# An attention and gated-MLP kernel: the order of work written by a recorder with a clock, and score banks refilled one by one

## The chip, the cores and the metric

One core of a Trainium2 chip. The metric is device time in microseconds, the median of several executions. Engine names as in the profile: PE is TensorE (PEld its weight loads), ACT is ScalarE, DVE is VectorE, POOL is GpSimd, SP is SyncE. All times in us unless marked ns.

## The reference

```
x  [1, 2048, 512] bf16;  wq [512, 32*16], wk, wv [512, 16], wo [512, 512], w1 [512, 1792], w2 [1792, 512]
xn = layernorm(x)
q  = (xn @ wq) as 32 heads of 16;  k = xn @ wk;  v = xn @ wv        # one k and one v for all heads
p  = softmax(q k^T / sqrt(16))                                      # [32, 2048, 2048]
s  = (p v, heads side by side) @ wo
g  = silu(silu(xn @ w1) @ w2)
out = x + s * g
```

The 32 x 2048 x 2048 exponentials are the bulk of the work. The second input called x is not used.

## The kernel before

The 2048 queries are four chunks (`c`) of 512; the 32 heads are eight groups (`g`) of four. A *group* below is one of the 32 pairs (c, g). Keys come in 16 tiles of 128 (`kt`). A *block* is one head's scores for one key tile and one chunk, transposed: 128 keys x 512 queries, one PSUM bank in fp32. So a key tile of a group has four blocks, one for each head `i`.

**Scores.** A head has 16 channels, so a block is a matmul that uses 32 of the array's 128 rows (L509); matmuls of different `i` run side by side. Two blocks at a time go into `psA0` or `psA1` (two banks each).

**Two ways to an exponential.** Most blocks are done by ScalarE: one ACTIVATE Exp of 128 x 1024, two blocks, from `psA` into `pa_sb` (L568). The others, called dense here, go by VectorE: a TENSOR_SCALAR adds a constant to the scaled score and clamps at zero, and the int16 result, read as bf16, is a coarse exponential, the first *pattern* (`ph0`, L581). GpSimd then makes two shifted patterns from it by INT64_ADD on four int16 at once (`ph1`, `ph2`, L592), and the three patterns together, each with its own weight, are the finer exponential.

**Values.** For each block of ScalarE's and each pattern, a matmul with 32 columns (16 value channels, and ones for the denominator) accumulates into `psO` (L628); four of them, one for each head, run side by side. When a group is complete, VectorE transposes `psO` (L663), takes the reciprocal (L668), multiplies (L674, into `onb_sb`) and, for every second group, transposes back (L679).

**The dense layer.** Matmuls for the MLP (L759, L771), the queries of later chunks (L393) and the output projection (L782) are *jobs* on the single bank `psF`. MLP results pass through a tanh on ScalarE (L817, `t_sb`) and a multiply on VectorE (L858), the output through L866 and the final add of x (L824), then a store on SP's queue. `warm` and `filler` (L268, L805) issue matmuls of zeros where TensorE would otherwise be idle.

**The order.** `Sched.op` records each operation with what it reads and writes; from that it derives the semaphores. Each engine executes its own list strictly in the order recorded. The order is a fixed pattern, written out by hand: `units` are ScalarE's key tiles, two exponentials each (`emit_E`), `dtiles` are the dense ones. A unit with a dense half takes two blocks of a dense tile, together, in `psD` (banks D and D1, one TENSOR_SCALAR of 128 x 1024 in `emit_P1`), and after the second half `emit_shift` issues GpSimd's two adds. After each score pack a rule chooses between a few packs of value matmuls (`emit_PV`) and a part of a job (`emit_job`, two or three matmuls). VectorE's small tasks are let in by `run_dve_task` as far as `room` allows: 0.85 us a unit, or 1.3 with a tanh, by the costs in `COST`, and tasks `gn3` (L674) and `add` (L824) only in every second unit:

```
while room > 0:
    k = run_dve_task(2 * u - 2, [t for t in ANY if COST[t] <= room and not (ph == 0 and t in ("gn3", "add"))])
    room -= COST.get(k, 9)
```

The first `NFRONT` = 12 units (24 exponentials) have no dense half; between them the normalisation and k and v of the later chunks are done. `x_sb` holds all 16 tiles of x from the start to the final add. The pattern buffers have three slots (`NPD`, `NPS`), `pa_sb` has eleven (`NPA`).

Of the kernel before, what the change touches and what calls it, by code (L numbers as in the profile page):

```python
# [35 lines left out]
class Sched:  # L36

    def __init__(self):
        self.queues = {}
        self.done = {}
        self.clock = {}
        self.snap = {}
        self.last_w = {}
        self.readers = {}
        self.flagged = {}
        self.lanes = {}

    def op(self, eng, fn, reads=(), writes=(), lane=None):
        who = lane or eng
        if lane:
            self.lanes[lane] = eng
        n = self.done.get(who, 0)
        self.done[who] = n + 1
# [15 lines left out]
        for w in writes:  # L72
            if w in self.last_w:
                dep(*self.last_w[w])
            for f, m in self.readers.get(w, {}).items():
                dep(f, m)
        clk = self.clock.setdefault(eng, {})
# [61 lines left out]
def bass_recurrent_scan__grouped_kv_mqa__dense_activation_silu__prompt_kernel(  # L139
# [25 lines left out]
    NPD = 3  # L165
# [6 lines left out]
    LEAD = 1  # L172
    NFRONT = 12

    with ExitStack() as es:
# [18 lines left out]
        ph_sb = [sb(f"ph{j}_sb", [P, NPD if j == 0 else NPS, 4 * NQ], I16) for j in range(NPH)]  # L194
# [37 lines left out]
        def load_x(a, b, queue="sp"):  # L232
            op(queue, lambda e: e.dma_start(x_sb[:, a:b, :], xv[:, a:b, :]), writes=[("x", t) for t in range(a, b)],  # L233
               lane=f"lx{a}")
# [7 lines left out]
        op("sp", lambda e: e.dma_start(wq_sb[:], A_wq.rearrange("(dc p) n -> p dc n", p=P)), writes=["wq"], lane="lwq")  # L242
# [22 lines left out]
        def warm(n, bank, key):  # L265
            def f(e):
                for _ in range(n):
                    r = e.matmul(bank, lhsT=zero_sb[:, 0:P], rhs=zero_sb[:, :], start=True, stop=True)  # L268
                return r
            op("pe", f, reads=["zero"], writes=[key])  # L270
# [119 lines left out]
        def mm_Q(c, t, dcs=range(NDC)):  # L390
# [5 lines left out]
            op("pe", f, reads=xnT_keys(c) + ["wq"], writes=["F"])  # L396

        def evac_Q(c, t, eng):
# [3 lines left out]
            else:  # L402
                op("v", lambda e: e.tensor_scalar(dst, psF[:, :], QSCALE, None, op0=ALU.mult), reads=["F"], writes=[("qT", c % 2, t)])
# [86 lines left out]
        units, dtiles = [], []  # L490
        for c in range(NC):
            for g in range(NG):
                n = 0
                while n < NKT and NFRONT + 2 * (len(dtiles) + n + 1) <= len(units) + (NKT - n - 1) - LEAD:
                    n += 1
                units += [(c, g, kt) for kt in range(NKT - n)]
                dtiles += [(c, g, kt) for kt in range(NKT - n, NKT)]
        NU = len(units)
        first_unit = [min(u for u, k in enumerate(units) if k[0] == c) for c in range(NC)]
        for u, k in enumerate(units):  # L500
            phase = (u - NFRONT) % 2
            m = (u - NFRONT) // 2
            d = dtiles[m] if u >= NFRONT and m < len(dtiles) else None
            units[u] = dict(phase=phase, pair=m, A=[[(k, 0), (k, 1)], [(k, 2), (k, 3)]][::1 if phase == 0 else -1],
                            D=[] if d is None else [(d, 0), (d, 1)] if phase == 0 else [(d, 2), (d, 3)])

        def score(e, blk, ap):
            (c, g, kt), i = blk
            return e.matmul(ap, lhsT=kT_sb[g % 2][32 * i:32 * i + 32, kt * P:(kt + 1) * P],  # L509
                            rhs=qT_sb[32 * i:32 * i + 32, c % 2, g // 2, :],  # L510
                            start=True, stop=True, tile_position=(32 * i, 0))

        def burst(items, writes):
            rd = set()
            for ((c, g, kt), i), _ in items:
                if ("q", c, g // 2) not in jst["q"]:
                    raise ValueError(f"no q for {c}, {g}")
                rd.add(("qT", c % 2, g // 2))
                rd.add(("kT", 1, kt // 2, i) if g % 2 else ("kT", 0, kt // 2 if kt else "first"))

            def f(e):
                for blk, ap in items:
                    r = score(e, blk, ap)
                return r
            op("pe", f, reads=sorted(rd, key=str), writes=writes)

        def emit_S(u, which):

            un = units[u]
            burst([(blk, psA[which][:, 512 * k:512 * k + 512]) for k, blk in enumerate(un["A"][which])], ["A%d" % which])  # L530
            if which == 1 and un["D"]:
                burst([(blk, psD[:, 512 * k:512 * k + 512]) for k, blk in enumerate(un["D"])], ["D", "D1"])

        NGRP = NC * NG
        pend = [[] for _ in range(NGRP)]
        left = [0] * NGRP
        for un in units:
            for blk in un["D"]:
                left[blk[0][0] * NG + blk[0][1]] += NPH
            for h in range(2):  # L540
                for blk in un["A"][h]:
                    left[blk[0][0] * NG + blk[0][1]] += 1
        npv = [[0] * 4 for _ in range(NGRP)]
        tot = [[0] * 4 for _ in range(NGRP)]
        for un in units:
            for blk in un["D"]:
                tot[blk[0][0] * NG + blk[0][1]][blk[1]] += NPH
            for h in range(2):
                for blk in un["A"][h]:
                    tot[blk[0][0] * NG + blk[0][1]][blk[1]] += 1  # L550

        step_now = [0]
        state = dict(g=0, o_step=-1, half=0)

        def fresh(key):
            for q in pend:
                for p in q:
                    if p["key"] == key:
                        raise ValueError(f"{key} is still to be read, step {step_now[0]}")

        def emit_E(u, h):
            un = units[u]
            if not un["A"][h]:
                return
            sl = (2 * u + h) % NPA
            step_now[0] = 2 * u
            fresh(("pa", sl))
            op("a", lambda e: e.activation(pa_sb[:, sl, :], psA[h][:, :], ACT.Exp, scale=ESCALE),  # L568
               reads=["A%d" % h], writes=[("pa", sl)])
            for k, (kk, i) in enumerate(un["A"][h]):  # L570
                gi = kk[0] * NG + kk[1]
                pend[gi].append(dict(i=i, kt=kk[2], v=0, ap=pa_sb[:, sl, 512 * k:512 * k + 512], key=("pa", sl),
                                     ready=2 * u + h))

        def emit_P1(u):
            un = units[u]
            if not un["D"]:
                return
            sl, h = un["pair"] % NPD, un["phase"]
            fresh(("ph", 0, sl, h))  # L580
            op("v", lambda e: e.tensor_scalar(ph_sb[0][:, sl, 1024 * h:1024 * h + 1024], psD[:, :],  # L581
                                              float(PH_ONE + PH_BIAS), 0.0, op0=ALU.add, op1=ALU.max),
               reads=["D", "D1"], writes=[("ph", 0, sl, h)])
            for k, (kk, i) in enumerate(un["D"]):
                ap = ph_sb[0][:, sl, 1024 * h + 512 * k:1024 * h + 512 * k + 512].bitcast(BF16)
                pend[kk[0] * NG + kk[1]].append(dict(i=i, kt=kk[2], v=1, ap=ap, key=("ph", 0, sl, h), ready=2 * u + 1))

        def emit_shift(u):
            sl, ss = units[u]["pair"] % NPD, units[u]["pair"] % NPS
            for j in range(1, NPH):  # L590
                fresh(("ph", j, ss))
                op("gp", lambda e, j=j: e.int64_add(ph_sb[j][:, ss, :].bitcast(I64), ph_sb[0][:, sl, :].bitcast(I64),  # L592
                                                    PH_SHIFT[j] * 0x0001000100010001),
                   reads=[("ph", 0, sl, 0), ("ph", 0, sl, 1)], writes=[("ph", j, ss)])
                for h in range(2):
                    for k, (kk, i) in enumerate(units[u - 1 + h]["D"]):
                        ap = ph_sb[j][:, ss, 1024 * h + 512 * k:1024 * h + 512 * k + 512].bitcast(BF16)
                        pend[kk[0] * NG + kk[1]].append(dict(i=i, kt=kk[2], v=1 + j, ap=ap, key=("ph", j, ss),
                                                             ready=2 * (u + 1) + j))

        def emit_PV(step, cap, may_end=True):
            gi = state["g"]
            if gi >= NGRP or step <= state["o_step"]:
                return 0
            n = 0
            while n < cap:
                cand = sorted((p for p in pend[gi] if p["ready"] <= step), key=lambda p: p["ready"])
# [6 lines left out]
                last = left[gi] <= sum(1 for _ in cand)  # L614
# [393 lines left out]
```

## Time and profile before

| | |
|---|---|
| median of 3 runs | 696.4 (695.93 to 697.16) |
| profiled execution, first to last instruction | 695.3 |
| ScalarE busy | 677.0, 97% |
| TensorE busy | 677.3, 97% (6279 matmuls) |
| VectorE busy | 552.4, 79% |
| GpSimd busy | 352.3, 51% |
| granted TensorE clock | 1.000 |
| HBM traffic | 6.85 MB read, 2.10 MB written |

The profile gives the span of one execution; what a timed run has beyond it is the difference of the first two rows, 1.1. Busy time counts an engine as busy while at least one of its instructions is in flight. Matmuls overlap and their ends are modelled, so TensorE's 97% says little of its reserve; its start-to-start distances say more. ScalarE and VectorE instructions overlap too, by a part of their length.

### The profile page before, as it was taken

The numbers are of one execution on the slowest core, as the hardware profiler recorded it, in microseconds if no ns is written. First come the engines' busy times: TensorE is split into PE (matmuls) and PEld (weight loads), VectorE is DVE, ScalarE is ACT, GpSimd is POOL, SyncE is SP. The second block draws the span as 40 slices with busy tenths as digits, with TensorE's granted clock in tenths as the row PEclk, the third lists the DMA queues.
The fourth block names the chain that finished last, engine by engine and source line by source line (L and its number), as shares of the span: only waits on it lengthen the run. The fifth ranks groups of instructions, "written<-read, shape, count | busy, mean of one in ns | idle before, by whom it ended". The sixth has DMA issues, their size and how long they took to land.

```text
span 695.3 us, 14435 instructions
## 1 busy us (share of the span) xinstructions
PE 677.3 (97%) x6279; PEld 183.0 (26%) x6279; DVE 552.4 (79%) x639; ACT 677.0 (97%) x773; POOL 352.3 (51%) x361
## 2 busy tenths in 40 slices
PE   8999999999999999999999999999999999999996
PEld 3432222222222222222222222222222222222221
DVE  6778778887778877888778787887878888787884
ACT  5899999999999999999999999999999999999995
POOL 4134545545455555555555555455545555555452
PEclk9999999999999999999999999999999999999999
DMA  9300000000000000000000000000000000000000
GB/s 296 112 5 1 1 2 1 1 1 2 1 1 8 9 1 9 8 2 1 1 1 10 8 8 1 10 1 1 1 2 1 8 17 2 9 1 2 1 1 31
DMA packets 7887, 10.13 MB, mean 15 GB/s; under 512 B 1744, under 2 KB 7120, under 8 KB 7824
## 3 DMA queue, kind: packets, MB, share of 16 engines
q1 hardware_dynamic: 6656, 5.15, 2.4%
q0 software_dynamic: 736, 3.67, 1.5%
q8 instruction: 49, 0.80, 0.5%
q10 hardware_dynamic: 432, 0.39, 0.2%
q14 instruction: 14, 0.11, 0.1%
HBM read 6.85 MB, written 2.10 MB: 13 GB/s over the span
## 4 chain that ended last, share of the span: by engine, by line
ACT 93%; PE 4%; DVE 1%; DMA 1%; POOL 0%; SPq 0%; issue 0%; DVEq 0%
ACT pa_sb L568 87%; ACT t_sb L817 5%; DMA wq_sb<-in_A_wq_dram 1%; PE psA L509 1%; PE psF L268 1%; PE psD L316 1%; DVE stats_sb L277 0%; PE psO L628 0%; POOL rstd_sb L286 0%; PE psD L351 0%; PE psF L351 0%; PE psA L939 0%; SPq L233 0%; PE psF L771 0%; DVE wq_sb L960 0%
## 5 line engine op out<-in xcount | busy, mean ns | idle before, releaser
L568 ACT ACTIVATE pa_sb<-psA 128x1024 bf16<-128x1024 f32 x692 | 660.5, 1233 | 4.3 <-PE psA L509 3.8
L592 POOL INT64_ADD ph_sb<-ph_sb x332 | 340.5, 1038 | 306.0 <-DVE ph_sb L581 306.0
L581 DVE TENSOR_SCALAR ph_sb<-psD 128x1024 int16<-128x1024 f32 x332 | 405.3, 1221 | 97.6 <-PE psD L509 96.5
L628 PE MATMUL psO<-ph_sb,vaug_sb 128*32 128x512 bf16 x1992 | 236.4, 384 | 0.0
L628 PE MATMUL psO<-pa_sb,vaug_sb 128*32 128x512 bf16 x1384 | 208.9, 384 | 0.4 <-ACT pa_sb L568 0.4
L509 PE MATMUL psA<-qT_sb,kTa_sb 32*128 32x512 bf16 x700 | 135.7, 384 | 4.5 <-ACT pa_sb L568 3.4
L509 PE MATMUL psA<-qT_sb,kTb_sb 32*128 32x512 bf16 x684 | 132.7, 385 | 3.5 <-ACT pa_sb L568 2.5
L509 PEld LDWEIGHTS psA<-qT_sb,kTa_sb 32*128 32x128 bf16 x700 | 32.9, 90 | 152.4 <-ACT pa_sb L568 146.5
L509 PEld LDWEIGHTS psA<-qT_sb,kTb_sb 32*128 32x128 bf16 x684 | 32.1, 91 | 152.0 <-ACT pa_sb L568 150.1
L628 PEld LDWEIGHTS psO<-ph_sb,vaug_sb 128*32 128x32 bf16 x1992 | 53.0, 94 | 58.1 <-issue 45.1
L759 PE MATMUL psF<-xnT_sb,w_sb 128*128 128x512 bf16 x224 | 67.8, 384 | 0.0
L509 PE MATMUL psD<-qT_sb,kTb_sb 32*128 32x512 bf16 x340 | 66.0, 384 | 0.0
L771 PE MATMUL psF<-w_sb,u_sb 128*128 128x512 bf16 x224 | 65.0, 384 | 0.0
L509 PE MATMUL psD<-qT_sb,kTa_sb 32*128 32x512 bf16 x324 | 62.8, 385 | 0.0
L628 PEld LDWEIGHTS psO<-pa_sb,vaug_sb 128*32 128x32 bf16 x1384 | 49.2, 94 | 43.9 <-issue 33.3
L817 ACT ACTIVATE t_sb<-psF 128x512 bf16<-128x512 f32 x72 | 59.3, 824 | 0.0
L858 DVE SCALAR_TENSOR_TENSOR u_sb<-t_sb,psF 128x512 bf16<-128x512 bf16 x56 | 38.3, 684 | 20.6 <-ACT t_sb L817 20.6
L268 PE MATMUL psF<-zero_sb 128*128 128x512 bf16 x100 | 34.3, 413 | 1.2 <-DVE zero_sb L252 1.2
L663 DVE STREAM_TRANSPOSE otr_sb<-psO 128x512 f32<-128x512 f32 x32 | 22.9, 715 | 5.4 <-PE psO L628 5.0
L771 PEld LDWEIGHTS psF<-w_sb,u_sb 128*128 128x128 bf16 x224 | 14.1, 97 | 25.6 <-issue 21.5
L393 PE MATMUL psF<-xnT_sb,wq_sb 128*128 128x512 bf16 x64 | 19.2, 384 | 1.1 <-DMA wq_sb<-in_A_wq_dram 1.1
L759 PEld LDWEIGHTS psF<-xnT_sb,w_sb 128*128 128x128 bf16 x224 | 12.7, 97 | 25.4 <-issue 24.7
(83 smaller groups left out, 222.6 us busy)
## 6 DMA issues: line engine op xcount, KB each, us to landing
w_sb<-in_B_w_dram POOLq DMA_DIRECT2D x2, 1792.0 KB, 12.9
out_dram<-ob_sb SPq DMA_DIRECT2D x15, 128.0 KB, 1.7
x_sb<-in_A_x_dram SPq DMA_DIRECT2D x3, 512.0 KB, 8.2
wq_sb<-in_A_wq_dram SPq DMA_DIRECT2D x1, 512.0 KB, 7.9
wop_sb<-in_A_wo_dram SPq DMA_DIRECT2D x1, 512.0 KB, 10.3
x_sb<-in_A_x_dram SPq DMA_DIRECT2D x2, 128.0 KB, 2.9
x_sb<-in_A_x_dram ACTq DMA_DIRECT2D x2, 128.0 KB, 3.1
kTb_sb<-kTa_sb SPq DMA_DIRECT2D x16, 16.0 KB, 3.0
```

The costliest lines, as they stand in the source:

```text
L268: r = e.matmul(bank, lhsT=zero_sb[:, 0:P], rhs=zero_sb[:, :], start=True, stop=True)
L393: r = e.matmul(psF[:, :], lhsT=wq_sb[:, dc, t * P:(t + 1) * P], rhs=xnT_sb[:, dc, c * NQ:(c + 1) * NQ], start=(dc == 0), stop=(dc == NDC - 1))
L509: return e.matmul(ap, lhsT=kT_sb[g % 2][32 * i:32 * i + 32, kt * P:(kt + 1) * P], rhs=qT_sb[32 * i:32 * i + 32, c % 2, g // 2, :], start=T ...
L568: op("a", lambda e: e.activation(pa_sb[:, sl, :], psA[h][:, :], ACT.Exp, scale=ESCALE), reads=["A%d" % h], writes=[("pa", sl)])
L581: op("v", lambda e: e.tensor_scalar(ph_sb[0][:, sl, 1024 * h:1024 * h + 1024], psD[:, :], float(PH_ONE + PH_BIAS), 0.0, op0=ALU.add, op1=A ...
L592: op("gp", lambda e, j=j: e.int64_add(ph_sb[j][:, ss, :].bitcast(I64), ph_sb[0][:, sl, :].bitcast(I64), PH_SHIFT[j] * 0x0001000100010001), ...
L628: r = e.matmul(psO[32 * i:32 * i + 32, :], lhsT=vaug_sb[:, p["v"], p["kt"], :], rhs=p["ap"], start=s0, stop=s1, tile_position=(0, 32 * i), ...
L663: op("v", lambda e: e.transpose(otr_sb[:, sl, :], psO[:, :]), reads=["O"], writes=[("otr", sl)])
L759: r = e.matmul(psF[:, :], lhsT=w1_sb[:, dc, ft * P:(ft + 1) * P], rhs=xnT_sb[:, dc, c * NQ:(c + 1) * NQ], start=(dc == 0), stop=(dc == NDC ...
L771: r = e.matmul(psF[:, :], lhsT=u_sb[:, (tt // 4) % 2, ft, (tt % 4) * P:(tt % 4 + 1) * P], rhs=w2_sb[:, ft, :], start=(ft == 0), stop=(ft = ...
L817: op("a", lambda e: e.activation(t_sb[:, sl, :], psF[:, :], ACT.Tanh, scale=0.5 if jb[0] == "h" else 0.25), reads=["F"], writes=[("t", sl)])
L858: op("v", lambda e: e.scalar_tensor_tensor(out=dst, in0=t_sb[:, sl, :], scalar=1.0, in1=psF[:, :], op0=ALU.add, op1=ALU.mult), reads=["F", ...
```

## The change

The mathematics, the instructions' kinds and the first 24 exponentials stay. What decides the order changes:

- **A clock in the recorder.** `op` takes a `cost`, and `model` books each operation on its engine: start, end, the time of a semaphore, of a change of tiling on TensorE, of ScalarE's overlap. `ready` tells when an operation's inputs will be there, `needed` when ScalarE's next scores must be issued.
- **A loop in place of the hand-written pattern.** In each step it lets VectorE's list advance to the present (`advance_v`, first come first served, with ages and a preference for blocks that TensorE needs soon), chooses how many packs TensorE can take before the next scores are needed (`slots`), fills them with values or a job, and issues the next scores (`score_run`). Which key tiles become dense is decided then: whenever a bank is free, `fill_D` takes a block.
- **Banks one by one.** D and D1 are refilled and read separately, by a TENSOR_SCALAR of 128 x 512 each; two ready neighbours may still go as one of 128 x 1024. `psF` is a third bank for blocks when no job wants it. Two dense key tiles may be open at a time.
- **A fourth pattern slot.** `NPD` = 4; the fourth slot of each pattern lies in x's tiles (0 to 11), which are free after the normalisation. x is therefore loaded again, tile by tile into tiles 12 to 15, four output tiles ahead of the final add (`load_xr`), on SP's queue.
- `gn3` and `add` are no longer tied to a position; they are booked at 0.43 and 0.42.

Counted in the built program: ScalarE has 678 exponentials (before 692) and 72 tanhs (72). VectorE has 692 dense blocks (664): 646 in single instructions and 46 in 23 pairs (before, 332 pairs). GpSimd has 346 pattern adds (332). TensorE has 3432 value matmuls (3376), 2048 score matmuls (2048) and 83 matmuls of zeros (115). SP has 16 loads of x more.

The core of the diff:

```diff
-    NPD = 3
+    NPD = 4
-    LEAD = 1
     NFRONT = 12
+    AGE2 = 12.0
+    KEEP, ENDQ, ROUND, MAXJOB, AHEAD, Q_EARLY = 0.6, 12, 3.0, 2, 3, 0.20
+    LEAD, LEAD_END, SLIP, AGE, AGE1, MARGIN = 3, 3, 0.15, 2.0, 1.2, 0.0
...
+    SWITCH, FLY, SEM = 0.104, 0.172, 0.048
...
+    def model(self, eng, lane, cost, r):
...
+        if eng == "a":
+            n = cost or 512
+            t = max(r, self.free["a"], self.act_end - 0.428)
+            self.free["a"] = t
+            self.act_end = max(t + 0.3 + n / 1200.0, self.act_end + 0.0635 + n / 1200.0)
+            return self.act_end + self.SEM
+        t = max(r, self.free[eng] - (0.084 if eng == "v" else 0.0))
+        self.free[eng] = t + (cost or 0.4)
+        return self.free[eng] + self.SEM
...
+        def ph_ap(j, sl, a, b):
+            if sl < 3:
+                return ph_sb[j][:, sl, a:b]
+            return x_sb[:, 4 * j:4 * j + 4, :].rearrange("p a b -> p (a b)").bitcast(I16)[:, a:b]
...
+        def exp_D(blks):
...
+            d = op("v", lambda e: e.tensor_scalar(ph_ap(0, sl, 512 * pos, 512 * pos + m), src,
+                                                  float(PH_ONE + PH_BIAS), 0.0, op0=ALU.add, op1=ALU.max),
+                   reads=[b["bank"] for b in blks], writes=[ph_key(0, sl, b["pos"]) for b in blks],
+                   cost=1.221 if len(blks) == 2 else 0.687)
...
+        def needed():
+            return K.act_end - 0.685 - MARGIN
...
+        def load_xr(tt):
+            if tt < NT:
+                op("sp", lambda e: e.dma_start(x_sb[:, 12 + tt % 4, :], xv[:, tt, :]), writes=[("x", 12 + tt % 4)],
+                   lane=f"xr{tt % 4}")
...
+        def fill_D(t, free):
+            banks = sorted(free_banks(t + SLIP), key=lambda b: (b == "F", K.ready("pe", [], [b])))
+            keep = 0
+            if "F" in banks and jobs and behind(F_BEHIND) and next_job(t):
+                keep = 1
+            for bank in banks[:max(0, len(banks) - keep)]:
+                pick = [(o, i) for o in dst["open"] for i in o["todo"] if i in free]
...
+                if not pick and len(dst["open"]) < 2:
+                    new = next_D(t)
...
+                burst([((o["tile"], i), bank_ap(bank))], [bank])
...
+        while state["g"] < NGRP or jobs or jst["open"] or tasks:
+            t = max(now, min(K.pe_next("col"), K.pe_next("full")))
...
+            advance_v(t + 0.05)
...
+            if tanh_ready(K.act_end - 0.33 if more else t):
+                emit_tanh()
...
+            if more:
+                last, aim = needed(), target(t)
+                slots = min(4, int((last - t - K.SWITCH) / 0.2163), max(0, int((aim - t - K.SWITCH) / 0.2163 + ROUND)))
...
+                dense_first = can and not full and not end and (jst["open"] or behind() or not more)
+                if dense_first:
+                    did = emit_job(t, slots)
+                if slots - did >= (2 if did else 1):
+                    did += emit_PV(max(t, K.pe_last + K.pe_len) + 0.08, slots - did - (1 if did else 0))
...
+                score_run(t)
```

## The prediction

> **What bounds the kernel now.** I read the page first (busy shares, then the chain that ended last), then ScalarE's and VectorE's lines in the timeline, then the waits.
>
> ```profile
> PE 677.3 (97%) x6279; PEld 183.0 (26%) x6279; DVE 552.4 (79%) x639; ACT 677.0 (97%) x773; POOL 352.3 (51%) x361
> ACT 93%; PE 4%; DVE 1%; DMA 1%; POOL 0%; SPq 0%; issue 0%; DVEq 0%
> L568 ACT ACTIVATE pa_sb<-psA 128x1024 bf16<-128x1024 f32 x692 | 660.5, 1233 | 4.3 <-PE psA L509 3.8
> L592 POOL INT64_ADD ph_sb<-ph_sb x332 | 340.5, 1038 | 306.0 <-DVE ph_sb L581 306.0
> L581 DVE TENSOR_SCALAR ph_sb<-psD 128x1024 int16<-128x1024 f32 x332 | 405.3, 1221 | 97.6 <-PE psD L509 96.5
> ```
>
> PE and ACT (ScalarE) both show 97%, but the chain is 93% ScalarE, and its 692 exponentials stood idle for only 4.3 us in all. The exponentials overlap (1233 ns each, yet closer together), so their price is the spacing. The chain, in order of time, and the timeline have it:
>
> ```profile
> 655.82 30.26 ACT pa_sb L568 x33
> 12.96 6.52 ACT L568 ACTIVATE pa_sb<-psA 128x1024 bf16<-128x1024 f32 x7 [2.01 <-PE psA L509]
> 302.66 0.88 ACT L817 ACTIVATE t_sb<-psF 128x512 bf16<-128x512 f32 x1
> 303.14 4.06 ACT L568 ACTIVATE pa_sb<-psA 128x1024 bf16<-128x1024 f32 x4
> 679.27 6.80 ACT L568 ACTIVATE pa_sb<-psA 128x1024 bf16<-128x1024 f32 x7
> ```
>
> 30.26/33 is 0.917 us per exponential; a tanh takes 0.48 (302.66 to 303.14). 692 x 0.917 + 72 x 0.48 = 669.2 us. The first exponential starts at 12.96, the last ends at 679.27 + 6.80 = 686.07, 673.1 later: all but 3.9 us is these two kinds, and those 3.9 lie in the first 60 us. So ScalarE's queue is the kernel, with a head of 13.0 and a tail of 9.3 us (686.07 to 695.3). The other engines matter only as far as they make ScalarE wait.
>
> **What the change takes from ScalarE.** The built order has 678 exponentials and 72 tanhs: 14 fewer, and 692 instead of 664 blocks of 128 keys x 512 queries on VectorE. Both orders are fixed when the program is built, so this is certain: 14 x 0.917 = 12.8 us less. Head and front phase (the first 24 exponentials) have the same score packs, and in the tail one pack of value matmuls follows the last exponential in both. If nothing new makes ScalarE wait, the span is 695.3 - 12.8 = 682.5. The median of the runs, 696.4, lies 1.1 above the span, and I carry that: 683.6 is the floor.
>
> **What it adds to VectorE.** The rows that price a dense block:
>
> ```profile
> 101.29 0.69 DVE L858 SCALAR_TENSOR_TENSOR u_sb<-t_sb,psF 128x512 bf16<-128x512 bf16 x1 [0.60 <-ACT t_sb L817]
> 101.89 1.22 DVE L581 TENSOR_SCALAR ph_sb<-psD 128x1024 int16<-128x1024 f32 x1
> 111.44 1.23 DVE L581 TENSOR_SCALAR ph_sb<-psD 128x1024 int16<-128x1024 f32 x1
> 112.58 0.68 DVE L858 SCALAR_TENSOR_TENSOR u_sb<-t_sb,psF 128x512 bf16<-128x512 bf16 x1
> L403 DVE TENSOR_SCALAR qT_sb<-psF 128x512 bf16<-128x512 f32 x16 | 11.0, 685 | 2.3 <-PE psF L393 1.8
> ```
>
> Each start lies some 0.08 before the end ahead of it: a pair of banks costs 1.14 us in a row (111.44 to 112.58), one bank about 0.60 (101.29 to 101.89; the nearest form, L403, lasts 685 ns). Before: 332 x 1.14 = 378.5. After: 646 singles and 23 pairs, 646 x 0.602 + 23 x 1.14 = 415.1. So VectorE gains 36.6 us: 552.4 + 36.6 = 589, 86% of 682.5 (counted in order against ScalarE's queue, 79 to 88% by stretch). Without any overlap the 646 singles cost 0.685 each and the share is 90%. On the path this is nothing, as long as a block is read before TensorE wants its bank again. GpSimd's pattern adds go from 332 to 346, 14 x 1.04 = 14.5 us in an engine at 51%: nothing.
>
> The Trainium skill (VectorE: DVE Perf Modes, The DRAIN you can't avoid) says that the next operation does not start until the pipe is empty, which speaks against splitting pairs; here the starts lie 0.08 before the ends, as its following section allows for instructions that are not held, so the trace sides with the overlap.
>
> **TensorE, which feeds ScalarE.**
>
> ```profile
> 680.63 0.39 PE L509 MATMUL psA<-qT_sb,kTb_sb 32*128 32x512 bf16 x2
> 680.95 0.39 PE L628 MATMUL psO<-pa_sb,vaug_sb 128*32 128x512 bf16 x2
> 681.18 0.38 PE L628 MATMUL psO<-pa_sb,vaug_sb 128*32 128x512 bf16 x2
> 681.54 0.39 PE L509 MATMUL psA<-qT_sb,kTb_sb 32*128 32x512 bf16 x2
> PEld psA L509 <- ACT pa_sb L568: 296.6, 663, 1.0
> ACT pa_sb L568 <- PE psA L509: 3.8, 5, 2.0
> ```
>
> A pack (four value matmuls side by side, or one dense matmul) comes 0.22 after one of its kind and 0.32 after one of another kind. One step, from one exponential's score pack to the next, with n packs in between, takes 0.64 + 0.22(n-1). After the front phase the order before has 1474 packs in 667 steps, 0.913 us a step by these prices; the order after has 1456 in 653 steps, 0.909 a step. ScalarE gives 0.917 and a tenth of a tanh, 0.97. So TensorE keeps 0.06 us a step, as before, 41 us in all, and in the trace it waited for ScalarE in 663 of its steps. But the spread grows: steps with three packs or more go from 103 to 211. Carried along in order at these prices, with a step's surplus handed on to the next, score packs would start behind their release in 410 steps instead of 219. How late may one be? The last matmul of a score pack starts 0.43 before its exponential can, and exponentials that started 0.10 before the end of the one ahead still lost nothing (they lasted 1017 ns, the minimum). With release at the end of the exponential before that, 0.33 us are free. By that carry one step in 653 exceeds it. So by its matmuls alone TensorE still hides.
>
> **New waits.** TensorE asked VectorE for a bank at 332 score packs; now at 598. Queued behind that wait on TensorE are the step's value and dense packs and the next exponential's scores. A late VectorE instruction can thus reach ScalarE. The planner places work by fixed durations; one row shows that a duration is not fixed:
>
> ```profile
> L674 DVE TENSOR_TENSOR onb_sb<-otr_sb,rcp_sb x32: 411/426/801, 54.8 to 687.6; 128x256 bf16<-128x256 f32 x32
> ```
>
> The normalising multiply (32 of them, booked at 0.43) lasts 0.80 where it meets a pattern add; the final add (12, booked at 0.42) likewise, mean 605 ns. The old order kept both out of every other step's room; the new one does not look at GpSimd, which is busy 54% of the time. 44 x 0.54 x 0.37 = 8.8 us of VectorE delay, in bits of up to 0.37. Bounds for what reaches ScalarE: 0 (VectorE has 14% and TensorE 0.06 a step to spare) and 8.8 (all of it); below zero is excluded, since nothing here shortens an exponential. I take a third, 3, as the bits exceed the free 0.33 only on steps already late. With 0.5 for small misfits (ScalarE lost 0.6 after 40 us before), the loss is 3.5: 682.5 + 3.5 = 686.0 span, **687.1** as time.
>
> The Trainium skill (Advanced Engine Details and Errata, GPSIMD Details) names a shared read and write interface and conflicts with VectorE instructions that have two SBUF inputs. By that rule alone each of the 44 that meets an add waits for its end, half of 1.04 on average, 44 x 0.54 x 0.52 = 12.4 us, an estimate from it; the sum above goes by the row.
>
> Costed at nothing: the x tiles as fourth slot need 16 reloads of 128 KB, 2.9 us each to landing on SP's queue, which holds only stores then; each is issued four output tiles ahead (for the last four, some 38 VectorE instructions or 23 us ahead). Without that cover one add would wait 2.9 us with VectorE's queue behind it. Two open tiles, the third bank and the finer pattern keys only add room. Fillers fall from 115 matmuls to 83, off the path; the clock row shows 9s throughout.
>
> **Rivals.**
> 1. *Nothing is lost*: 683.6. For it: before, all engines were this full and ScalarE lost 0.6 us after 40 us. Against: banks are now asked for nearly twice as often. 20%.
> 2. *TensorE bound through the dense banks (slower)*: TensorE stands at the bank for w us in each step. It has 0.062 to spare, so 653 x (w - 0.062) reaches ScalarE; the 12.8 are gone at w = 0.082, and w = 0.10 gives 683.6 + 24.8 = 708. For it: 598 waits, a VectorE at 86% and single blocks on banks that are refilled at once. Against: VectorE waited 96.5 us for TensorE's dense scores, not the other way round. 15%.
> 3. *VectorE's instructions do not overlap, or its delays add up*: VectorE at 90% and more, ScalarE losing 9 to 14 us: 693 to 698, about no change. The overlap rows speak against it. 9%.
> 4. *Others* (a tanh placed ahead of an exponential before its bank is full; a stretch in the last 60 steps, where no tanh gives TensorE room): 4%, 690 to 700.
>
> That the change does not do what it says is excluded by the built order.
>
> **How the numbers follow.** The forecast (loss 1 to 8 us, 684.6 to 692) has 52%. The range runs from the floor, 683.5, to 699, into rival 2's lower half; left out are about 12% above and 3% below. A measurement of this kernel tells about 0.2%, 1.4 us: faster is below 695.0. Forecast and rival 1 make 72%, a third of rivals 3 and 4 makes 4 more: faster 0.77; same 0.06 (middle of rival 3, edge of 2); slower 0.17 (most of 2, and the rest of 3 and 4).
>
> **What would show it.** Right: 678 exponentials at 0.917, the line ACT pa_sb <- PE psA at about 4 to 12 us, single-bank evacuations at 0.685 and VectorE near 86%. The normalising multiply at a mean near 0.6. Wrong: ScalarE's idle time above 15 us with TensorE's weight loads for psD waiting for VectorE, or a chain in which VectorE or TensorE holds more than a tenth.

## The result, and the profile after

| | before | after |
|---|---|---|
| median | 696.16 (695.66 to 697.16, 4 runs) | 684.86 (684.39 to 686.25, 4 runs) |
| profiled execution, span | 695.3 | 682.9 (its time 684.74) |
| ScalarE / VectorE / GpSimd busy | 677.0 / 552.4 / 352.3 | 665.0 / 589.6 / 369.3 |
| granted TensorE clock, mean | 1.000 | 0.996 |

The ratio is 0.9837, interval 0.9822 to 0.9851: faster by 11.3 us. The forecast was 687.1.

The page of the changed kernel: the busy row, the chain that ended last, and the row of the exponentials.

```profile
PE 640.3 (94%) x6224; PEld 185.9 (27%) x6303; DVE 589.6 (86%) x976; ACT 665.0 (97%) x759; POOL 369.3 (54%) x375
ACT 88%; PE 7%; DVE 3%; DMA 0%; POOL 0%; issue 0%; DVEq 0%
L606 ACT ACTIVATE pa_sb<-psA 128x1024 bf16<-128x1024 f32 x678 | 644.4, 1189 | 3.9 <-PE psA L577 2.0
```

TensorE's 640.3 is too low: 6224 matmuls are recorded beside 6303 weight loads, so 79 records are missing here. ScalarE still holds 88% of the chain. Its 678 exponentials stood idle for 3.9 us in all (4.3 before), and VectorE's 589.6 is the sum that was forecast.

VectorE's groups with shapes kept apart show what a bank by itself costs:

```profile
L628 DVE TENSOR_SCALAR ph_sb<-psD 128x512 int16<-128x512 f32 x446 | 300.0, 682 | 42.4 <-PE psD L577 33.9 <-PE psF L577 3.3
L628 DVE TENSOR_SCALAR x_sb<-psD 128x512 int16<-128x512 f32 x144 | 97.9, 684 | 14.1 <-PE psD L577 12.8
L628 DVE TENSOR_SCALAR ph_sb<-psD 128x1024 int16<-128x1024 f32 x18 | 22.0, 1220 | 7.4 <-PE psD L577 7.4
```

The rows that write `x_sb` are the fourth pattern slot. One bank takes 682 or 684 ns, as the nearest row of before said (685).

The waits, by total:

```profile
PEld psA L577 <- ACT pa_sb L606: 261.9, 606, 0.8
DVE ph_sb L628 <- PE psD L577: 41.3, 139, 1.6
DVE x_sb L628 <- PE psD L577: 14.0, 51, 0.7
PEld psA L577 <- issue: 11.1, 35, 0.8
```

TensorE's score packs waited for ScalarE 606 times. VectorE waited 41 us for dense scores of the first three slots and 14 us for those of the fourth, together 55 (97 before): there was less slack, but VectorE was still the one that waited. The last row is the one to watch in the experiments: a score pack that waits for no one is one that comes late.

**Where the time went.** From the end of one of ScalarE's instructions to the end of the next, an exponential takes 0.917 and a tanh 0.49 (0.48 in the prediction). The count at these prices is called work here, and what a step takes beyond its price is a loss. The profiled execution of before: head 12.96, work 692 x 0.917 + 72 x 0.49 = 669.8, losses 3.16, tail 9.27 and 0.1 for the first exponential's own length; together 695.3. After: head 11.84, work 657.0, losses 4.73, tail 9.25, the same 0.1; together 682.9. So the work fell by the 12.84 that 14 exponentials cost, the head by 1.12, and the losses grew by 1.57: 3.1 in the front phase in both, then 0.27 in the middle (0.07 before) and 1.35 after 655 us (none before).

The middle's loss is one event of 0.48; the other steps there come out a little under their prices. The timeline around it (start, duration, instruction, idle time before it):

```profile
215.06 2.06 POOL L639 INT64_ADD ph_sb<-ph_sb  x2 [2.23 <-DVE ph_sb L628]
216.17 1.22 DVE L726 TENSOR_TENSOR onb_sb<-otr_sb,rcp_sb 128x256 bf16<-128x256 f32 x1
217.31 1.27 DVE L628 TENSOR_SCALAR ph_sb<-psD 128x512 int16<-128x512 f32 x2
218.04 0.38 PE L577 MATMUL psD<-qT_sb,kTb_sb 32*128 32x512 bf16 x1 [0.39 <-DVE ph_sb L628]
```

A normalising multiply starts 0.10 after the second of two pattern adds has started (each lasts 1.04) and lasts 1.22 instead of 0.41, to 0.28 after that add's end; the dense bank behind it in VectorE's queue is read late; TensorE stands 0.39 at that bank with the next scores queued behind it; ScalarE's exponential at 219.34 comes 0.48 late. That is the mechanism of the prediction, link by link, once. It is no accident of one execution: four runs below that keep this order (the first two doses, and more and fewer zeros) lose 0.47 to 0.49 at the same place, 220 to 221 us.

The end's loss was not in the prediction. Busy time by stretch (length, PE, PEld, DVE, ACT, POOL, then the granted clock):

```profile
655.00:660.00 5.00, 3.59 (x44) 1.09 (x44) 4.82 (x9) 5.00 (x6) 3.88 (x4) 1.00 0.00 0
660.00:662.00 2.00, 2.00 (x18) 0.24 (x10) 1.40 (x3) 1.87 (x3) 1.44 (x2) 0.50 0.00 0
```

From 659.97 to 663.38 the clock record shows 0.5. In the five microseconds ahead of it TensorE was busy for 3.59. Matmuls then last 0.60 instead of 0.39, and ScalarE loses 1.36.

### The profile page after: what moved, and what is told of

It is laid out like the page before. It is cut to its first block, busy times and chain, and to the rows that moved or that the text cites. A ratio compares the mean times of both kernels' runs of the same rounds, so it can differ in the third digit from the quotient of the medians.

```text
span 682.9 us, 14794 instructions
## 1 busy us (share of the span) xinstructions
PE 640.3 (94%) x6224; PEld 185.9 (27%) x6303; DVE 589.6 (86%) x976; ACT 665.0 (97%) x759; POOL 369.3 (54%) x375
## 4 chain that ended last, share of the span: by engine, by line
ACT 88%; PE 7%; DVE 3%; DMA 0%; POOL 0%; issue 0%; DVEq 0%
ACT pa_sb L606 83%; ACT t_sb L882 5%; PE psA L577 2%; PE psO L676 2%; DVE stats_sb L338 1%; PE psF L844 1%; PE psF L329 0%; DVE ph_sb L628 0%; DMA x_sb<-in_A_x_dram 0%; PE psD L377 0%; DVE xn_sb L369 0%; POOL rstd_sb L347 0%; PE psD L412 0%; PE psF L412 0%; DVE kTa_sb L424 0%
## 5 line engine op out<-in xcount | busy, mean ns | idle before, releaser
L639 POOL INT64_ADD ph_sb<-ph_sb x260 | 268.7, 1046 | 214.6 <-DVE ph_sb L628 214.6
L628 DVE TENSOR_SCALAR ph_sb<-psD 128x512 int16<-128x512 f32 (+1 forms) x464 | 321.9, 703 | 49.8 <-PE psD L577 41.3
L676 PE MATMUL psO<-ph_sb,vaug_sb 128*32 128x512 bf16 x1560 | 204.0, 385 | 0.4 <-ACT pa_sb L606 0.2
L639 POOL INT64_ADD x_sb<-x_sb x86 | 89.0, 1047 | 63.1 <-DVE x_sb L628 63.1
L577 PE MATMUL psD<-qT_sb,kTb_sb 32*128 32x512 bf16 x327 | 120.1, 386 | 0.4 <-DVE ph_sb L628 0.4
L628 DVE TENSOR_SCALAR x_sb<-psD 128x512 int16<-128x512 f32 (+1 forms) x149 | 104.0, 702 | 15.2 <-PE psD L577 14.0
L577 PE MATMUL psD<-qT_sb,kTa_sb 32*128 32x512 bf16 x309 | 112.0, 384 | 0.0
L676 PE MATMUL psO<-x_sb,vaug_sb 128*32 128x512 bf16 x516 | 92.9, 386 | 0.1
L577 PEld LDWEIGHTS psD<-qT_sb,kTb_sb 32*128 32x128 bf16 x327 | 28.3, 91 | 0.9 <-DVE ph_sb L628 0.7
L676 PEld LDWEIGHTS psO<-x_sb,vaug_sb 128*32 128x32 bf16 x516 | 23.1, 95 | 16.0 <-issue 11.2
```

The source lines that it names most:

```text
L628: d = op("v", lambda e: e.tensor_scalar(ph_ap(0, sl, 512 * pos, 512 * pos + m), src, float(PH_ONE + PH_BIAS), 0.0, op0=ALU.add, op1=ALU.ma ...
L639: d = op("gp", lambda e, j=j: e.int64_add(ph_ap(j, sl, 0, 2048).bitcast(I64), ph_ap(0, sl, 0, 2048).bitcast(I64), PH_SHIFT[j] * 0x00010001 ...
L676: r = e.matmul(psO[32 * i:32 * i + 32, :], lhsT=vaug_sb[:, p["v"], p["kt"], :], rhs=p["ap"], start=s0, stop=s1, tile_position=(0, 32 * i), ...
```

## The experiments

All start from the changed kernel.

**One part undone at a time.** Three runs show what each part of the change brings, and whether time follows the count of exponentials.

```diff
-    NPD = 4
+    NPD = 3                                        # e1: no slot in x's tiles
-                if not pick and len(dst["open"]) < 2:
+                if not pick and len(dst["open"]) < 1:   # e2: one open key tile
-            banks = sorted(free_banks(t + SLIP), ...)
+            banks = sorted([b for b in free_banks(t + SLIP) if b != "F"], ...)   # e3: no third bank
```

> The changed kernel with three pattern slots instead of four; its loop then places 694 exponentials on ScalarE (678) and 660 dense blocks on VectorE. Counting theory: the time is a head, 0.917 us for each exponential, 0.49 for each tanh and a tail, so 16 exponentials more cost 14.7: 684.9 + 14.7 = 699.6, or 698.2 if the clock dip near the end does not occur. Rival, by waits: the change won by sparing ScalarE waits as well, so undoing a part brings idle time too, over 3 us beyond the count, 702.6 or more.

> The changed kernel with one open dense key tile instead of two; 688 exponentials. Counting theory: 684.9 + 10 x 0.917 = 694.1 (692.7 without the clock dip). Rival by waits: 697 or more.

> The changed kernel without the dense layer's bank as a third score bank; 698 exponentials. Counting theory: 684.9 + 20 x 0.917 = 703.2 (701.8 without the clock dip). Rival by waits: 706 or more.

| | exponentials | by count, 684.86 + 0.917 each | measured | ratio to before |
|---|---|---|---|---|
| three slots | 694 | 699.5 | 699.95 (698.58 to 700.33) | 1.0055 [1.004, 1.007] |
| one open tile | 688 | 694.0 | 694.99 (693.37 to 699.01) | 0.9992 [0.9972, 1.0011] |
| two banks | 698 | 703.2 | 702.77 (701.84 to 703.9) | 1.01 [1.0085, 1.0115] |

Each lies within 1 us of its count. So the gain goes through one channel, the exponentials that ScalarE no longer does, and none of the three parts can be left out: without the third bank, or without the fourth slot, the new order is slower than the old one, and with one open tile it takes the same time. What a part would bring if it were added alone to the old order was not run. Ten executions with one open tile spread over 5.6 us, from 693.4 at a mean granted clock of 0.998 to 0.999 up to 699.0 at 0.990.

**Both banks together.** D and D1 are filled only when both are free, and read as a pair wherever they hold neighbours.

```diff
-                    if d2 <= d + 0.1 and meets(d + 0.735) >= meets(d2 + 1.27):
-                        d, blks = d2, two
+                    d, blks = d2, two
...
+            if not ("D" in banks and "D1" in banks):
+                banks = [b for b in banks if b == "F"]
```

> The changed kernel with D and D1 refilled only when both are free, and read as a pair of 128 x 1024 where they belong to one tile (196 pairs, 256 singles); 700 exponentials. Counting theory: 684.9 + 22 x 0.917 = 705.1 (703.7 without the clock dip). Rival by waits: 708 or more. A third view, that single refills are not what matters since VectorE's work per block is dearer with them, would have this kernel near 690.

Measured: 711.81 (710.3 to 714.56), ratio 1.0233 [1.0207, 1.026]. It has 700 exponentials, by count 705.0; 6.8 are lost on top. ScalarE's losses in its profiled execution are 7.2 us after the front phase (1.6 in the changed kernel) though VectorE is busy for only 551.0, so it is not the amount of VectorE's work that costs. That execution took 710.3, 5.3 over its count, and 5.6 is the growth of the losses. So the rival by waits (708 or more) was right here and the counting theory was not, and the view that single refills do not matter (690) is ruled out. Most of the extra is the clock: there are four stretches of 3.41 us at half clock, and about 4.7 of the 7.2 us are lost in them or within 3 us behind them. The first of them, and the stretch ahead of it, in which TensorE had little to do:

```profile
110.00:113.80 3.80, 2.03 (x19) 0.58 (x19) 3.79 (x6) 3.80 (x5) 2.18 (x4) 1.00 0.00 0
113.80:117.20 3.40, 3.40 (x13) 0.62 (x11) 2.29 (x5) 2.68 (x4) 0.96 (x1) 0.50 0.00 0
```

**How far does VectorE's reserve reach?** Each of the 669 dense evacuations is followed by a zeroing of a dead buffer on VectorE. It is not booked, so the order on every engine stays. Four widths were run; the edit is that of the second:

```diff
+            state["dose"] = state.get("dose", 0) + 1
+            op("v", lambda e, q=state["dose"] % 4: e.memset(wkp_sb[:, q, :], 0.0),
+               writes=[("dose", state["dose"] % 4)], cost=0.084)
```

> The changed kernel, same order, with a memset of 128 x 6 on VectorE behind each of the 669 dense evacuations, of which the recorder's clock knows nothing. It should add about 0.06 us each in a row, 40 us, VectorE's share from 86 to 92%. Cover theory (a bank is ready early enough, so small delays are absorbed): under 3 us more, 685 to 688. Rival 2 of the prediction (TensorE has 0.06 us a step and is already at the bank): most of the delay beyond that reaches ScalarE, 10 us or more, 695 up.

> As the kernel with the small dose, but a memset of 128 x 64 words, about 0.10 to 0.13 us each in a row, 70 to 85 us in all: VectorE at 95 to 99%. Cover theory: now the cover must be used up, since VectorE's own sum comes near ScalarE's 675: 10 to 30 us more, 695 to 715. If the time stays below 690, VectorE's reserve is larger than its busy share says.

> The changed kernel in the same order, with a zeroing of 128x128 words on VectorE after each of the 669 dense evacuations, not booked. The 128x64 one lasted 0.112 us, added 27 us to VectorE's busy time and nothing to the time; this one should last about 0.17 and add about 0.10 a block, 65 us: VectorE at 655, 96%. Theory 'VectorE's lateness is covered until its own sum passes ScalarE's': 684 to 690. Rival 'stretches that are already full lose': VectorE stood at 79 to 88% by stretch in the changed kernel, now 88 to 98%; then 692 to 705.

> The same with 128x256 words, about 0.27 us each, some 0.20 a block: 134 us more on VectorE, 723 us of work, more than ScalarE's 673.7. VectorE must become the bound and the chain must show it: 723 and its idle head and ends (about 20) give 735 to 755. If the time stays under 710, the zeroings still overlap with the evacuations and the dose is again smaller than meant.

| one zeroing | VectorE busy | loss after the front phase | measured | ratio to before |
|---|---|---|---|---|
| none | 589.6 | 1.6 | 684.86 | 0.9837 [0.9822, 0.9851] |
| 63 ns | 597.4 | 0.6 | 684.97 (684.0 to 687.37) | 0.9841 [0.9821, 0.9862] |
| 112 ns | 616.7 | 0.7 | 685.72 (683.85 to 686.58) | 0.9851 [0.9835, 0.9868] |
| 165 ns | 646.7 | 7.6 | 691.74 (690.57 to 692.77) | 0.9935 [0.992, 0.995] |
| 272 ns | 706.7 | 51.9 | 736.45 (735.06 to 739.51) | 1.0584 [1.0557, 1.061] |

The expectations of the first two doses had the amount wrong, and that of the second missed the time too: a zeroing overlaps so much with its neighbours that 63 ns added 0.012 a block instead of 0.06, and 112 ns 0.04 instead of 0.10 to 0.13. The two larger ones were added to reach what it had not. 27 us more on VectorE in even bits cost nothing that shows; 57 us cost 7; 117 us make VectorE the bound. The chains of the last two rows, in that order:

```profile
ACT 47%; PE 35%; DVE 16%; issue 0%; POOL 0%; DMA 0%; DVEq 0%
```

```profile
DVE 72%; PE 18%; ACT 8%; issue 1%; POOL 1%; DMA 0%; DVEq 0%
```

At 94% (165 ns) ScalarE holds only 47% of the chain (88% in the changed kernel), yet neither of the two expected bands, 684 to 690 and 692 to 705, was hit: the losses come in 46 bits of 0.05 to 0.6, in groups, in only part of the stretches between 116 and 678 us. This comes close to the prediction's second rival, and its waits show how it looks when it does happen:

```profile
PEld psA L577 <- ACT pa_sb L606: 228.6, 550, 0.8
PEld psA L577 <- issue: 28.4, 81, 0.6
```

81 score packs now wait for no one, 35 in the changed kernel, while TensorE's single waits for VectorE stay short (the longest in that run's rows for `psD` is 0.7 us). TensorE is not stopped for long anywhere; it is a little late too often.

**The same work in lumps.** The disputed term of the sum was the collision of VectorE's two-operand operations with the pattern adds. This run adds 83 such operations to the 44 of the changed kernel, again with the order unchanged.

```diff
+            if state["dose"] % 8 == 0:
+                op("v", lambda e: e.tensor_tensor(wkp_sb[:, :, :].rearrange("p a b -> p (a b)"),
+                   zero_sb[:, :], zero_sb[:, :], ALU.add), reads=["zero"], writes=[("dose", 0)], cost=0.084)
```

> The changed kernel in the same order, with one more addition of two SBUF operands (128x512 bf16, zeros, into a dead buffer) on VectorE after every eighth dense block, 83 in all, not booked. The changed kernel has 44 such operations; this makes 127. By the prediction's step (0.54 of them meet a pattern add, 0.37 each, a third of it reaches ScalarE) 83 more give 16.6 us of delay beside their own 0.42 each, and 5.5 us of time: 690.4. By what the changed kernel's trace showed (one collision of 44 reached ScalarE, about 0.5 us) they give about 1: 686. The two-operand rows should show a minimum near 0.42 and a longest over 1.

Measured: 693.82 (692.77 to 696.81, 10 runs), ratio 0.9967 [0.9957, 0.9978]: 9.0 above the changed kernel, more than either theory gave; the two executions with a clock of 1.000 took 692.8, still 7.9 above. The answer for the tile that they write has the lengths (shortest, median, longest):

```profile
L634 DVE TENSOR_TENSOR wkp_sb<-zero_sb x83: 396/416/1210, 45.8 to 678.4; 128x512 bf16<-128x512 bf16 x83
```

36 of the 83 last over 0.5 us; the mean is 0.578, so the collisions add 83 x 0.16 = 13.4 us (0.54 x 0.37 gave 16.6). VectorE is busy for 622.5, 33 more than in the changed kernel. The 112 ns zeroings had added 27 in even bits and cost nothing, and the 165 ns ones 57 and cost 7. So VectorE's sum alone does not decide what reaches ScalarE; how long a single delay is matters too. Whether a lump of 0.41 that meets no add would do the same was not run. The timeline of one of its large losses, as a chain:

```profile
385.23 0.41 DVE L634 TENSOR_TENSOR wkp_sb<-zero_sb 128x512 bf16<-128x512 bf16 x1
385.41 2.30 POOL L643 INT64_ADD ph_sb<-ph_sb  x2 [1.65 <-DVE ph_sb L628]
385.56 1.26 DVE L730 TENSOR_TENSOR onb_sb<-otr_sb,rcp_sb 128x256 bf16<-128x256 f32 x1
387.47 0.39 PE L577 MATMUL psD<-qT_sb,kTb_sb 32*128 32x512 bf16 x1 [0.26 <-DVE ph_sb L628]
388.07 0.82 PE L848 MATMUL psF<-xnT_sb,w_sb 128*128 128x512 bf16 x3 [0.21 <-DVE u_sb L918]
389.25 1.02 ACT L606 ACTIVATE pa_sb<-psA 128x1024 bf16<-128x1024 f32 x1 [0.84 <-PE psD L577]
```

Behind the added 0.41 the normalising multiply starts 0.15 after a pattern add has started; it lasts 1.26; TensorE waits once for a dense bank and once for the MLP's multiply, both queued behind it on VectorE; the next scores go out at 388.82, and the exponential at 389.25 comes 0.95 late. Such losses of 0.05 to 1.2, 41 of them, make 12.4 us after the front phase, 3.4 of them in the last 30 us, where this execution also had its clock at 0.5 from 668.31 to 675.14.

**The clock.** Two runs from opposite sides. In the first, 11 more matmuls of zeros go into gaps of the last two groups, not booked; in the second, the 44 matmuls of zeros in the loop are cut to two columns (163 ns instead of 379), booked as before. Neither changes the rest of the order.

```diff
+                elif idle > 0 and group_A() >= NGRP - 2 and K.activity(...) < 0.8 and ...:   # first
+                    filler(idle, False)
...
-                        r = e.matmul(psO[:, :], lhsT=zero_sb[:, 0:P], rhs=zero_sb[:, :], ...)
+                        r = e.matmul(psO[:, 0:2], lhsT=zero_sb[:, 0:P], rhs=zero_sb[:, 0:2], ...)   # second
```

> The changed kernel with 11 more matmuls of zeros, put into gaps of TensorE in the last two groups; nothing else in the order differs. Theory of the clock: the granted clock falls to half for 3.4 us near 660 because TensorE had too little to do before; ScalarE lost 1.4 us there. With the gaps filled the granted clock stays at 1.000 until the last store, the loss goes, and the time is 683.5, 0.998 of the changed kernel. Rival: the loss there comes from the thin last group (banks and patterns), so clock or not it stays, 684.9; or the zeros delay score packs and cost up to 1 us.

> The changed kernel in the same order, with the 44 matmuls of zeros in the loop cut from 512 columns to 2 (those ahead of the loop and in the tail stay). Theory 'the zeros hold the clock': TensorE's thin stretches are no longer filled, the granted clock falls to 0.5 in several windows of 3.4 us, as at 660 in the changed kernel, and each costs ScalarE 0.5 to 1.4: 687 to 695 and a mean clock of 0.97 to 0.99. Rival 'fillers are off the path and cost nothing', as the prediction had it: 684.9 and no new dip.

With more zeros: 684.30 (684.16 to 684.98), ratio 0.9828 [0.9814, 0.9843], mean clock 0.998 to 1.000 in its four runs (0.994 to 0.997 in those of the changed kernel). The profiled execution has no half-clock stretch before the tail:

```profile
655.00:660.00 5.00, 3.91 (x44) 1.03 (x41) 4.76 (x10) 5.00 (x7) 3.87 (x4) 1.00 0.00 0
660.00:662.00 2.00, 2.00 (x33) 0.50 (x25) 2.00 (x3) 2.00 (x3) 1.02 (x2) 1.00 0.00 0
```

But ScalarE still lost 0.8 us near there, so less than half of the 1.36 came back, and the two ratios' intervals overlap. It is the fastest version run here, by 0.6 us that the measurement does not separate from nothing. With fewer zeros: 685.21 (684.5 to 686.18), ratio 0.9843 [0.9828, 0.9857], clock 0.993 to 0.997: no different from the changed kernel, and the theory that the zeros hold the clock missed for these 44. Its profiled execution has one half-clock stretch too, but at another place, 437.32 to 440.73, and none at 660:

```profile
436.00:440.00 4.00, 3.54 (x17) 0.78 (x17) 3.44 (x7) 3.29 (x5) 3.30 (x4) 0.66 0.00 0
```

**A plan with fewer exponentials still.** The constants of the clocked recorder are moved (among them the delay it allows for an exponential's start, 0.3 to 0.18, and a preference against starting `gn3` and `add` while GpSimd adds), with the added zeros of the first clock run: 676 exponentials.

> A version meant to be faster: the recorder's clock lets an exponential start as late as the trace shows (0.18 instead of 0.30 us ahead of its data), the normalising multiply and the final add are placed when no pattern add runs, other constants found by search over the order, and the zeros of the end as in the warm-end kernel; 676 exponentials. Counting theory: 684.9 - 2 x 0.917 - 1.4 (clock) - 0.5 (the one collision) = 681.2. Rival: with the tighter clock, steps miss by a few 0.01 us and ScalarE loses what the count wins, 683 to 686.

Measured: 685.80 (685.26 to 686.03), ratio 0.9847 [0.9832, 0.9862]. Two exponentials are 1.8 us less; in its profiled execution the tail grew from 9.25 to 10.52, and the losses after the front phase were 2.1 instead of 1.6. The head was 12.80 instead of 11.84, in the range of the other runs (11.4 to 12.8). Together these are 2.7 us, so the 1.8 was given back and 0.9 more. The time is the rival's (683 to 686), but not by steps that miss by a few 0.01 us: 1.7 of the 2.1 were lost in the last 23 us, in bits of up to 0.28 and at full clock. The preference did what it was for: 5 of the 48 multiplies and adds last over 0.5 us (14 in the changed kernel), the longest 0.67, and the loss at 219 us is gone. Other constants were moved with it, so it is not isolated.

## Why the prediction was right, and where it was not

**Right: the count.** 14 exponentials left ScalarE's queue, their pace is 0.917 in both profiles, and the three undone parts and their counts confirm the price to 1 us: 14 x 0.917 = 12.84.

**Right: VectorE.** 589 forecast, 589.6 measured; 646 singles at 0.685 in length and 0.60 in a row; of all this one delay of 0.48 us reached ScalarE, told below. (The rival share of 90% prices the old pairs without overlap too; from their measured cost it would be 94%. Both are excluded.)

**Right: TensorE.** Late score packs were put at 410 by the carry; 415 of the changed kernel's 678 score packs start over 0.1 us after the end of the exponential that releases them, 394 of them after the front phase (before: 248 and 232, where the carry had 219). ScalarE lost nothing by their matmuls alone.

**Right in kind, wrong in size: "I take a third, 3".** The step that fails is the term of the sum for what reaches ScalarE. Four things in it were off. The share of two-operand operations that are lengthened to over 0.5 us by an add is 14 of 48 (the tail's four counted), not 0.54. The delay they add is 25.1 - 48 x 0.415 = 5.2 us, not 8.8. It is not new either: in the profile of before 18 of the 48 last over 0.5 us and the delay is 5.9 us, so the old order did not keep them apart. And the bits are not "of up to 0.37": four of the 14 are longer, three of 0.48 to 0.49 and one of 0.80. Of the 14 one reached ScalarE, with 0.48 us: the one of 0.80. The two rows of the normalising multiply, before and after, with the same mean:

```profile
L674 DVE TENSOR_TENSOR onb_sb<-otr_sb,rcp_sb 128x256 bf16<-128x256 f32 x32 | 16.8, 526 | 0.5
L726 DVE TENSOR_TENSOR onb_sb<-otr_sb,rcp_sb 128x256 bf16<-128x256 f32 x32 | 16.9, 527 | 0.1
```

So two of the signs named for "right" did not show: the multiply's mean is not near 0.6, and ScalarE's row `ACT pa_sb <- PE psA` has 2.0 us, not 4 to 12. That the reserve on VectorE and TensorE takes up the others fits the zeroings, of which it absorbs 27 us in even bits. Of the "0.5 for small misfits" nothing is seen: no other loss between 46 and 655 us is above 0.05. So rival 1, nothing lost (20%), was nearer to what happened than the forecast (52%): 683.6 and 687.1 around 684.86.

**Why the step was not foolish.** The run with 83 more collisions lost 9 us where the same step gave 5.5. There the operations were not booked, so their whole length came on top. What the case does not settle is how much of the changed kernel's small loss is due to the order leaving 0.43 for these operations, and how much to chance: no run removed only the booking.

**Missed: the end.** "Fillers fall from 115 to 83, off the path; the clock row shows 9s throughout." The row still shows 9s, in forty slices of 17 us, and hides a half-clock stretch of 3.4 us that cost this execution 1.36 us. That fewer zeros caused it is not shown: cutting 44 more to two columns changed nothing in time or mean clock. Shown is that zeros placed in the thin stretch at the end remove it; the last section ties it to how busy TensorE is in one window of 3.41 us.

**Mis-sized: the ends.** The prediction added 1.1 to its span, the median less the profiled execution's span. Where both numbers are known for one execution the difference is 1.8 to 2.2 us (684.74 and 682.9 here), so the profiled execution of before took about 697.1, longer than its median, which is why the spans differ by 12.4 us and the medians by 11.3. It had a head of 12.96 where 10 of the 13 later profiles have 11.4 to 12.2. The account of the 2.2 us by which 687.1 was too high: head -1.12, losses -1.93 (3.5 forecast, 1.57 measured), around the span +0.70, median over profiled execution +0.12.

**The rivals.** TensorE bound through the dense banks (15%) did not come, but its price is now known: it begins between 27 and 57 us of evenly spread VectorE work on top, or at the latest with 33 us in lumps, so the changed kernel stood 5 to 10% of VectorE's work away from it. No overlap on VectorE (9%) is excluded by the rows: 589.6, not 90%.

## What to carry to other kernels

When one engine's queue is the kernel, price a change by the instructions that it takes off that queue; then spend the doubt on whether the feeders are late by *one long* delay, not on the sum of their small ones. Here 27 us of extra feeder work in 0.04 us bits cost nothing, 57 us in bits of 0.085 cost 7, and 33 us in bits of 0.4 to 1.2 cost 9. And take the span from several executions, or at least compare the profiled one with the median, before carrying what lies around it.

## What the hardware showed that was not expected

- **The clock drops in the middle of a full kernel.** Every half-clock stretch inside the loop lasted 3.41 or 6.83 us, and its place changed with the kernel: 660 in the changed one, 437 with fewer zeros, 361 with three slots, 359 and 670 with one open tile, 470 with two banks, 668 with the added operations, 709 with the largest dose, and four places with paired banks; none in the profiled executions of before, of the three smaller doses, of the version with more zeros or of the replanned one. TensorE was not idle ahead of them, only thin (3.59 of 5.00 and 2.03 of 3.80 us busy). Those of 3.41 us cost ScalarE 1.1 to 1.4, the longer ones up to 2.7 (the largest dose, where VectorE is the bound, left out). The Trainium skill (TensorE: Matmul & The Clock Gate, Part 1: The HAM clock gate) gives a free-running window of about 3.4 us and half speed after an idle one; the lengths and the wandering place agree with it, but no idle window is seen ahead of them here.
- **What is seen ahead of them is a thin window.** Within one execution all half-clock stretches begin on one grid of 3.413 us, and where that grid lies differs from execution to execution. Cut on this grid, from 45 us to the last exponential, the 14 profiled executions have about 2600 windows at full clock. In eleven of them TensorE's matmul records fill less than two thirds (0.48 to 0.66), and half clock follows each of the eleven. Of all the others (0.69 and more) it follows one: 0.78, in the run with fewer zeros. The thin stretch near 655 to 660 us is the example. In the changed kernel a window of the grid takes most of it (2.21 of 3.42 us, first row); with the 112 ns doses, in the same order, the grid splits it in two (2.55 and 2.90 of 3.4 us, last two rows), and the clock stays. This is read off the traces; only the two clock runs changed the share on purpose (with more zeros the window from 655.24 has 2.79 of 3.41 us, and full clock behind it).

```profile
656.55:659.97 3.42, 2.21 (x25) 0.75 (x29) 3.42 (x7) 3.42 (x5) 2.33 (x3) 1.00 0.00 0
654.94:658.35 3.41, 2.55 (x33) 0.72 (x30) 3.31 (x11) 3.41 (x5) 2.37 (x3) 1.00 0.00 0
658.35:661.77 3.42, 2.90 (x35) 0.74 (x32) 3.42 (x10) 3.42 (x5) 2.37 (x3) 1.00 0.00 0
```

- **A two-operand VectorE operation that starts during one of GpSimd's adds is held until that add ends.** It lasts 0.41 us alone; the 14 long ones of the changed kernel end 0.27 to 0.28 us after the add they meet, so one add makes it anything up to 1.22 (1.26 with the added operations), by how early in the add it starts. An add that follows at once can stretch: most last 1.04, several 1.20, the longest 1.31.
- **A small write behind an evacuation is almost free.** A zeroing of 63 ns adds 0.012 to VectorE's busy time, one of 112 adds 0.04, 165 adds 0.085, 272 adds 0.175: 0.05 to 0.1 of each lies under its neighbours.
